# Moving one batch's query load, one transpose and two stores in the transfer order of a fused attention and MLP kernel

## Chip, core and metric

The kernel runs on one core of one Trainium2 chip. The metric is the device time of one launch in microseconds (us), taken several times; the median is the figure that is compared.

## What is computed

The reference is a linear attention without softmax, normalised per head, followed by a two-layer MLP with a sigmoid-approximated GELU:

```python
kv  = np.einsum('bhsd,bhse->bhde', k, v)          # b=8, h=8, s=576, d=64
out = np.einsum('bhsd,bhde->bhse', q, kv)
rms = np.sqrt(np.mean(out * out, axis=-1, keepdims=True) + 1e-06)
out = out / rms * g_norm
x = out.transpose(0, 2, 1, 3).reshape(4608, 512)
h = x @ w_in                                      # 512 x 2048
g = h * (1.0 / (1.0 + np.exp(-1.702 * h)))
return g @ w_out                                  # 2048 x 512, result float32
```

Inputs are float32 in HBM; the kernel computes in float16 with float32 sums.

## The kernel before

**Tiles and layers.** The 4,608 token rows are taken as nine tiles of 512 rows. Tiles 0 to 7 are the first 512 rows of batches 0 to 7; tile 8 gathers the remaining 64 rows of every batch. A loop over the tile number `t` (L982) writes one "layer" each time: both matrix products of the MLP for tile `t`, and, woven between their matmuls, the attention of batch `b = t + 1`, which yields the next layer's input `xT[b]`. The first product of a layer (L584 from layer 1 on) works through a list of steps; the second (L704) counts its 112 matmul positions `n` from 0 to 111. Layer 0 uses L473 and L819 with its own count. From layer 1 on both products use a seven-product scheme in place of eight block products.

**Order by hand.** The order is written out: `at1(i, f, ...)` hangs a call behind step `i` of the first product, `at2(n, f, ...)` behind position `n` of the second. Calls hung on one position run in the order in which they were hung. Each engine works through its own instructions in that order and waits where data is missing.

**Loads** are issued by GpSimd (POOL), which also casts float32 to float16 on the way; they use queue q0. `load_kv(b)` (L112) issues the 512 main rows of k and v into `kraw` and `vbuf`, then the 64 remaining rows of each. `load_q(b)` (L142) issues three transfers: the main rows of q, into `qbuf` for an odd batch and `qraw` for an even one, and two of 32 KB into `qrem[b % 2]`. There is one `kraw` and one `vbuf`, so k and v of the next batch can be loaded only when the products k-transposed times v (`kvp`, L247) of the batch before have read them.

**Turning.** SyncE (SP) issues DMA transposes, which go through queue q1 together with its stores. `transpose_q` (L288) turns q of batch b into `qTd`, of which there is one buffer; `transpose_rest` (L292) turns `qrem` into `qTr`. The products `outR` (L332, method `rows`) read `qTd`, the products `outT` of L306 read `qTr`. When the normalised result is in `x16`, `turn` (L359) multiplies it on VectorE and issues, after parts 1 and 3, a transpose into the next layer's `xT` (L368).

**Stores.** The result of tile `t` is collected in `osbs[t]`, with two buffers that alternate. Tiles 0 and 1 (`t < EARLY`) have another row order, so `store_early` (L838) issues eight transfers each of 64 to 192 KB, 1 MB in all, on SP; it is called at the end of `layers` (L797). Tiles 2 to 5 are stored in halves from within the second product (L692, L850), tiles 6 and 7 whole at the layer's end.

**Order around the change, before.**

| Where | What is hung there |
| --- | --- |
| layer 0, position 51 | clear the unused rows; `load_kv(2)`, second half of the heads and the remaining rows |
| end of layer 0 | `store_early(0)` on SP |
| layer 1, step 5 | `start(2)`, `transpose_q(2)`, `transpose_rest(2)` on SP |
| layer 1, step 22 | `load_kv(3)`, then `load_q(3)` |
| layer 1, positions 40, 50, 51, 52 | `turn` of batch 2, parts 0 to 3 |
| layer 1, positions 88 and 89 | k, v products of batch 3; `load_kv(4)`, `load_q(4)` |
| layer 1, position 100 | `transpose_q(3)`, `transpose_rest(3)` on SP |
| end of layer 1 | `store_early(1)` on SP |
| layer 2, position 15 | k, v products of batch 4, then `rows` of batch 3 |
| layer 2, positions 35, 38, 46, 48 | `turn` of batch 3 |
| layer 2, position 49 | `transpose_q(4)` on SP |
| layer 2, position 101 | v of batch 5 behind the end of batch 3's turning, q of batch 5 behind batch 4's `qTd` (POOL waits by a one-element copy, `mark`) |

Of the kernel before, what the change touches and what calls it, by code (L numbers as in the profile page):

```python
# [12 lines left out]
P = 128  # L13
# [3 lines left out]
def kernel(  # L17
# [10 lines left out]
    nc = tc.nc  # L28

    B, H, S, D = q.shape  # L30
# [7 lines left out]
    J = SM // P  # L38
    R = S - SM
    assert R == 64 and B * R == SM and KO == NPAIR and 2 * D == P  # L40
    NT = B + 1
    EARLY = 2
# [22 lines left out]
    qrem = [const.tile([P, 2, P], F16, name=f"qrem{i}") for i in range(2)]  # L65
# [71 lines left out]
    def q_rows(b):  # L137

        rows = qbuf if b % 2 else qraw.rearrange("p c x -> p (c x)")
        return rows[:, 0 : H * J * D]  # L140
# [14 lines left out]
    for n in "kqv":  # L155
# [11 lines left out]
        out=ident,  # L167
        in_=ident,
# [52 lines left out]
    class Attention:  # L221
# [63 lines left out]
                    r = slice(hl * D, (hl + 1) * D)  # L285
                    copy(self.engine, self.kb[to, c0:c1, half, 1 - hl], self.kvp[r, c0:c1, :])

        def transpose_q(self):  # L288
            self.qTd = attn.tile([P, H * J // 2, P], F16, name="qTd", tag="qTd", bufs=1)
            nc.sync.dma_start_transpose(out=self.qTd, in_=q_rows(self.b))  # L290

        def transpose_rest(self):  # L292
# [489 lines left out]
    def layers(t, units1, units2):  # L782
        hid = d0 if t == 0 else Hidden(t)
        seven = Seven(t, hid.gT) if t else None
        left = hid_seven(t, hid, seven, units1) if t else first_columns(hid, units1)
        osbs[t] = opool.tile([P, 4, DM], F32, name="osb", tag="osb")
        if t:
            todo = {n: [lambda x=x: seven.sums(*x) for x in xs] for n, xs in plan(t).later.items()}
            for n, us in units2.items():
                todo.setdefault(n, []).extend(us)  # L790
            for n, us in left.items():
                todo[n] = us + todo.get(n, [])
            seven.run(todo)
        else:
            project_all(hid.gT, units2)
        if t < EARLY:
            store_early(t)  # L797
        elif t < B and t not in HALVED:
            store(t, 0, J)

    def first_columns(hid, units):

        for i, fo in enumerate(COLS):
            if i >= GROUP:
                for ko in range(KO):
                    hid.mm(ko, fo)
                hid.gate(fo)
            for u in units.get(i, ()):
                u()
# [28 lines left out]
    def store_early(t):  # L838
        n = 0
        while n < SM:  # L840
            mo, j, p = n // P, n // PE_, n % PE_
            m = min((mo + 1) * P, (j + 1) * PE_) - n
            nc.sync.dma_start(
                out=out[t * S : (t + 1) * S, :][bass.DynSlice(NJ * p + j, m, step=NJ), :],
                in_=osbs[t][n % P : n % P + m, mo, :],
            )
            n += m

    def store(t, j0, j1):
        nc.sync.dma_start(  # L850
            out=out[t * S : t * S + SM, :].rearrange("(p j) m -> p j m", j=J)[:, j0:j1],
            in_=osbs[t][:, j0:j1],
        )
# [119 lines left out]
    def plan(t):  # L973
        return SECOND if t < EARLY else LATER if t < B - 1 else LAST_TWO

    HALVED = (2, 3, 4, 5)
# [5 lines left out]
    for t in range(NT):  # L982
        b = t + 1
        u1, u2 = {}, {}

        def at1(i, f, *args):
            u1.setdefault(i, []).append(lambda: f(*args))

        def at2(i, f, *args):
            u2.setdefault(i, []).append(lambda: f(*args))  # L990

        def of(b, name, *args):
            return lambda: getattr(live[b], name)(*args)

        if t == 0:
            for l in range(2):
                at1(6, nc.vector.memset, kvd[l], 0.0)
            at1(7, of(0, "out", NPAIR))
            at1(7, scale_w_in, 0, 4)
            at1(7, w_in_sums, 0, 2)  # L1000
            at1(8, start, 1)
            at1(12, scale_w_in, 4, 6)
            at1(12, w_in_sums, 2, 3)
            at1(13, load_q, 2)
            at2(4, setattr, a0, "ss_pool", Attention.ss_pool)
            at2(4, of(0, "ss", NPAIR, True))
            at2(4, of(0, "apply", NPAIR))
            at2(18, weight_sum, 0, 0, HF)
            at2(18, scale_w_in, 6, 8)
            at2(18, w_in_sums, 3, 4)  # L1010
            for c in range(NPAIR):
                at1(12, of(1, "pack_q", c))
                at2(9 + 3 * c, of(1, "q", c))
                at2((36, 36, 49, 49)[c], of(1, "kv", c))
                at2((41, 43, 54, 55)[c], of(1, "out", c))
                at2((45, 50, 58, 60)[c], of(1, "ss", c))
                at2((48, 52, 58, 62)[c], of(1, "apply", c))
            for n in range(1, 4):
                at2(19, weight_sum, n, 0, 4)
                at2(38, weight_sum, n, 4, 6)  # L1020
            at2(39, load_kv, 2, 0, H // 2, False)
            at2(51, clear_rest)
            at2(51, load_kv, 2, H // 2, H)

            def first_sum():
                made[1] = Sums(1, xT[1])
                made[1].form(0)

            at2(55, first_sum)
        elif b < B:  # L1030
            todo = plan(t)
            at = todo.attn
            if t == 1:
                at1(todo.steps.index("kv"), of(b, "kv_all", "D"))
                at1(5, start, b)
                at1(5, of(b, "transpose_q"))
                at1(5, of(b, "transpose_rest"))
                at1(4, nc.scalar.preload_act_table_set, "gelu_apprx_sigmoid_and_others")
                for n, i in ((1, 8), (2, 11), (3, 16)):
                    at1(i, weight_sum, n, 6, HF)  # L1040
                at1(22, load_kv, 3)
                at1(22, load_q, 3)
                at2(88, start, 3)
                at2(88, of(3, "kv_all", "A"))
                at2(89, load_kv, 4)
                at2(89, load_q, 4)
            elif t + 2 < B:
                at2(at["rows"][0], start, t + 2)
                at2(at["rows"][0], of(t + 2, "kv_products"))
                at2(52, of(t + 2, "kv_copies", "A"))  # L1050
                if t + 3 < B:
                    at2(at["rows"][0], load_kv, t + 3, 0, H, False, "k")
                    at2(101, after_turn, b)
                    at2(101, load_kv, t + 3, 0, H, True, "v")
                    at2(101, after_queries, t + 2)
                    at2(101, load_q, t + 3)
            if t + 2 < B:
                at2(49 if t > 1 else 100, of(t + 2, "transpose_q"))
                at2(100, of(t + 2, "transpose_rest"))
            at2(at["table"], nc.scalar.preload_act_table_set, "abs_reciprocal_sqrt_and_small")  # L1060
            for h in range(2):
                at2(at["roots"][h], of(b, "roots", h))
            for j in range(J):
                if j < J // 2:
                    at2(at["rows"][j], of(b, "rows", j))
                for name in ("add_up", "turn"):
                    at2(at[name][j], of(b, name, j))
            rest = (80, 90, 96, 97) if 1 < t < B - 2 else (46, 74, 80, 82)
            at2(rest[0], of(b, "out", NPAIR))
            at2(rest[1], of(b, "ss", NPAIR))  # L1070
            at2(rest[2], of(b, "apply", NPAIR))
            at2(rest[3], nc.scalar.preload_act_table_set, "gelu_apprx_sigmoid_and_others")
        elif t < B:
            for name in ("ss_pool", "rest_pool"):
                at2(16, setattr, live[1], name, (ps_a, "att"))
            at2(16, of(1, "out", NPAIR))
            at2(34, nc.scalar.preload_act_table_set, "abs_reciprocal_sqrt_and_small")
            at2(44, of(1, "ss", NPAIR))
            at2(50, of(1, "apply", NPAIR))
            at2(52, nc.scalar.preload_act_table_set, "gelu_apprx_sigmoid_and_others")  # L1080
        layers(t, u1, u2)


# [28 lines left out]
```

## Time and profile before

| What | Value |
| --- | --- |
| median of 3 runs | 259.14 us |
| lowest and highest | 258.35 and 259.88 us |
| the profiled execution's own time | 259.74 us |
| its span, first to last instruction | 258.0 us |
| mean granted TensorE clock | 0.993 of full speed |
| read from HBM, written | 36.70 MB, 9.44 MB |

The profile shows one execution. Its times are counted from the first instruction; 1.74 us of the profiled execution's time lie outside the span. Engines are PE (TensorE matmul), PEld (its weight loads), DVE (VectorE), ACT (ScalarE), POOL (GpSimd) and SP (SyncE). The layers stand in the chain of work as follows: layer 0 ends at 47.96 us, layer 1 at 75.30, layer 2 at 101.42, layer 3 at 127.54; later layers follow in steps of 26.1 to 24.5 us, and the last matmul ends at 254.30.

A row of a timeline gives start, duration, engine, line, operation and count. For a DMA this is the time its engine took to issue it, not that of the transfer. A row of DMA issues gives the size and, at its end, the time from issue to landing. A row of DMA queues gives packets, MB and the share of 16 engines' time in the stretch asked for; a share over 100% means that packets overlapped.

### The profile page before, as it was taken

How to read it: one execution, taken by the hardware profiler on the slowest of the kernel's cores; microseconds unless marked ns; L12 is line 12 of the kernel's file. 1: busy time of each engine (PE TensorE's matmuls, PEld its weight loads, DVE VectorE, ACT ScalarE, POOL GpSimd, SP SyncE). 2: the span in 40 equal slices, each digit the busy share in tenths (PEclk: the TensorE clock that was granted, in tenths of full speed). 3: DMA queues.
4: the chain of work that ended last, by engine and by line, in shares of the span. 5: the costliest groups of instructions: out<-in, count | busy, mean ns of one | idle time of the engine just before them, and what ended most of it. 6: DMA issues, size and time to landing. Idle time of an engine off the chain costs nothing.

```text
span 258.0 us, 6355 instructions
## 1 busy us (share of the span) xinstructions
PE 251.7 (98%) x2596; PEld 204.4 (79%) x2596; DVE 193.9 (75%) x344; ACT 177.1 (69%) x322; POOL 57.0 (22%) x92
## 2 busy tenths in 40 slices
PE   8899999999999999999999999999999999999994
PEld 2444454788888888888888888898888888888883
DVE  1546685899958986798679867987799787857872
ACT  3458743988758894899579957995799469536800
POOL 8773244208061013301150134000000000000013
PEclk9979999999999999999999999999999999999999
DMA  7999999999989979996999699909500430012005
GB/s 181 194 188 206 204 204 197 216 216 115 184 159 208 221 91 224 153 158 81 186 184 164 84 205 135 190 5 136 202 4 0 84 163 3 0 57 108 3 19 145
DMA packets 68687, 35.33 MB, mean 137 GB/s; under 512 B 37970, under 2 KB 66258, under 8 KB 68402
## 3 DMA queue, kind: packets, MB, share of 16 engines
q0 software_dynamic: 37632, 18.31, 55.3%
q1 hardware_dynamic: 30624, 16.29, 27.4%
q8 instruction: 20, 0.33, 0.5%
q10 hardware_dynamic: 402, 0.33, 0.5%
q14 instruction: 9, 0.07, 0.1%
HBM read 36.70 MB, written 9.44 MB: 179 GB/s over the span
## 4 chain that ended last, share of the span: by engine, by line
PE 93%; DMA 4%; issue 0%; POOL 0%; DVE 0%
PE o L704 38%; PE h L584 38%; PE hT L473 6%; PE o L819 5%; DMA vbuf<-in_v_dram 2%; DMA qraw<-in_q_dram 2%; PE kvp L247 2%; PE outR L332 1%; PE ss L379 1%; PE outT L302 1%; PE q L454 0%; PE kvp L259 0%; PE outT L306 0%; PE kv L259 0%; DVE osb L684 0%
## 5 line engine op out<-in xcount | busy, mean ns | idle before, releaser
L561 ACT ACTIVATE gT<-h 128x512 f16<-128x512 f32 x96 | 52.5, 601 | 5.6 <-PE h L584 5.6
L584 PEld LDWEIGHTS <-ws 128*128 128x128 f16 x512 | 50.1, 98 | 5.9
L704 PEld LDWEIGHTS <-gS 128*128 128x128 f16 x512 | 49.1, 98 | 6.1 <-DVE gS L636 0.3
L584 PE MATMUL h<-xS,ws 128*128 128x256 f16 x384 | 52.2, 273 | 0.0
L704 PE MATMUL o<-tw,gS 128*128 128x256 f16 x384 | 45.6, 273 | 0.0
L584 PEld LDWEIGHTS <-w_in_sb 128*128 128x128 f16 x384 | 37.4, 98 | 4.7
L704 PEld LDWEIGHTS <-gT 128*128 128x128 f16 x384 | 37.6, 98 | 4.3
L704 PE MATMUL o<-w_out_sb,gT 128*128 128x256 f16 x256 | 31.4, 273 | 0.0
L584 PE MATMUL h<-xT,w_in_sb 128*128 128x256 f16 x224 | 31.1, 272 | 0.0
L681 DVE TENSOR_TENSOR osb<-o,qf 128x512 f32<-128x512 f32 (+1 forms) x25 | 16.7, 669 | 11.7 <-PE o L704 11.7
L598 DVE TENSOR_TENSOR h<-h,s 128x512 f32<-128x512 f32 x32 | 22.2, 698 | 4.2 <-PE h L584 2.6
L600 DVE TENSOR_TENSOR s<-h,s 128x512 f32<-128x512 f32 x32 | 22.1, 691 | 4.1 <-PE h L584 3.3
L738 POOL DMA_DIRECT2D out_dram<-osb x6 | 3.2, 537 | 93.2 <-DVE osb L681 93.2
L636 DVE TENSOR_TENSOR gS<-gT 128x512 f16<-128x512 f16 (+2 forms) x32 | 21.3, 685 | 0.6 <-ACT gT L561 0.6
L561 ACT ACTIVATE gT<-s 128x512 f16<-128x512 f32 x32 | 19.8, 628 | 2.4 <-DVE s L600 2.3
L530 DVE COPY s<-h 128x512 f32<-128x512 f32 x19 | 13.0, 686 | 8.2 <-PE h L584 8.2
L584 PE MATMUL h<-xS,w_in_sb 128*128 128x256 f16 x128 | 18.9, 273 | 0.0
L115 POOL DMA_DIRECT2D kraw<-in_k_dram x7 | 6.0, 853 | 56.9 <-PE kvp L247 52.0
L348 DVE TENSOR_REDUCE sum<-sq 128x8 f32<-128x512 f16 x24 | 14.9, 678 | 4.7 <-ACT sq L342 4.7
L320 ACT ACTIVATE sq<-outT 128x512 f16<-128x512 f32 (+1 forms) x16 | 7.9, 495 | 15.1 <-PE outT L302 9.5
L990 ACT ACT_TABLE_LOAD x14 | 18.0, 1283 | 0.2
L381 ACT ACTIVATE rs<-ss,eps_t 128x512 f32<-128x512 f32 (+1 forms) x16 | 9.2, 582 | 12.4 <-PE ss L379 12.3
(104 smaller groups left out, 373.9 us busy)
## 6 DMA issues: line engine op xcount, KB each, us to landing
out_dram<-osb SPq DMA_DIRECT2D x8, 512.0 KB, 4.6
kraw<-in_k_dram POOLq DMA_DIRECT2D x5, 512.0 KB, 6.0
vbuf<-in_v_dram POOLq DMA_DIRECT2D x5, 512.0 KB, 10.4
out_dram<-osb SPq DMA_DIRECT2D x2, 1024.0 KB, 4.9
qraw<-in_q_dram POOLq DMA_DIRECT2D x3, 512.0 KB, 11.6
qbuf<-in_q_dram POOLq DMA_DIRECT2D x3, 512.0 KB, 10.4
out_dram<-osb SPq DMA_DIRECT2D x6, 192.0 KB, 5.9
w_in_sb<-in_moe_w_in_dram POOLq DMA_DIRECT2D x2, 512.0 KB, 10.1
```

The lines of the kernel that those rows point to most:

```text
L348: nc.vector.tensor_reduce(out=self.sum4[:, j, :], in_=self.o[j][1].rearrange("p (x d) -> p x d", d=D), op=ALU.add, axis=mybir.AxisListType.X,)
L473: nc.tensor.matmul(self.h[fo], w_in_sb[:, ko, fo * P : (fo + 1) * P], self.x[:, ko], start=(ko == 0), stop=(ko == KO - 1),)
L530: (nc.vector.tensor_copy if engine == "D" else nc.scalar.copy)(to, src)
L561: nc.scalar.activation(self.gT[:, to, n * TH : (n + 1) * TH], src, AFT.Gelu_apprx_sigmoid)
L584: nc.tensor.matmul(bank[name][:, a], w, x, start=(p in (1, 5) and a == 0 and k == 0), stop=(k == KH - 1), skip_group_check=True,)
L598: nc.vector.tensor_add(bank["z"], bank["x"], self.s5)
L600: nc.vector.tensor_add(self.s5, bank["x"], self.s5)
L636: op(s[:, n, lo], a, b)
L681: nc.vector.tensor_add(o, ps, self.kept[with_][:, m])
L704: nc.tensor.matmul(o, a, w, start=(p in (1, 2, 5) and i == 0 and (mo == 0 or split)), stop=(i == HF - 1), skip_group_check=True,)
L819: nc.tensor.matmul(os[mo], gT[:, fo, mo * P : (mo + 1) * P], w_out_sb[:, fo, :], start=(fo == 0), stop=(fo == FO - 1),)
L990: u2.setdefault(i, []).append(lambda: f(*args))
```

## The change

`load_q(3)` moves from layer 1, step 22, to layer 0, position 51, behind the last load of batch 2's k and v. `transpose_q(2)` gets a one-column copy on GpSimd ahead of it: it reads the last column of `qrem[1]`, which the last two transfers of `load_q(3)` fill, and writes into `qTd`, so the transpose, which overwrites `qTd`, comes behind it. `store_early(0)` moves from the end of layer 0 to layer 1, position 53, one behind the last part of batch 2's turning; `store_early(1)` moves from the end of layer 1 to layer 2, position 49, behind `transpose_q(4)`, which is hung on the same position earlier in the text. `at["turn"][J - 1] + 1` is 53 in layer 1 and 49 in layer 2.

```diff
-        def transpose_q(self):
+        def transpose_q(self, after=None):
             self.qTd = attn.tile([P, H * J // 2, P], F16, name="qTd", tag="qTd", bufs=1)
+            if after is not None:
+                nc.gpsimd.tensor_copy(out=self.qTd[0 : 2 * R, 0, 0:1], in_=after)
             nc.sync.dma_start_transpose(out=self.qTd, in_=q_rows(self.b))
...
-        if t < EARLY:
-            store_early(t)
-        elif t < B and t not in HALVED:
+        if EARLY <= t < B and t not in HALVED:
             store(t, 0, J)
...
             at2(51, load_kv, 2, H // 2, H)
+            at2(51, load_q, 3)
...
                 at1(5, start, b)
-                at1(5, of(b, "transpose_q"))
+                at1(5, of(b, "transpose_q", qrem[1][0 : 2 * R, 1, P - 1 : P]))
                 at1(5, of(b, "transpose_rest"))
...
                 at1(22, load_kv, 3)
-                at1(22, load_q, 3)
...
             at2(rest[3], nc.scalar.preload_act_table_set, "gelu_apprx_sigmoid_and_others")
+            if b - 2 < EARLY:
+                at2(at["turn"][J - 1] + 1, store_early, b - 2)
```

## The prediction

> **What bounds the kernel now.** I read the page first, then the sums by layer, the chain of waits, and last the timelines of the two engines that issue transfers.
>
> ```profile
> span 258.0 us, 6355 instructions
> PE 251.7 (98%) x2596; PEld 204.4 (79%) x2596; DVE 193.9 (75%) x344; ACT 177.1 (69%) x322; POOL 57.0 (22%) x92
> ```
>
> ```profile
> 47.96:75.30 27.34, 27.34 (x343) 23.67 (x342) 24.87 (x46) 21.93 (x41) 7.61 (x10) 1.00 1.25 182
> 75.30:101.42 26.12, 26.12 (x303) 23.27 (x302) 21.00 (x35) 20.59 (x39) 4.88 (x9) 1.00 1.13 173
> ```
>
> TensorE sets the time: in layers 1 and 2 its busy time (second number) equals the length of the stretch (first). No transfer ends a wait of TensorE there, so an earlier transfer buys nothing; a later one costs only if it passes its deadline. The deadlines are in the chain of waits:
>
> ```profile
> 63.33 0.57 PE outR L332 x32
> ...
> 67.12 0.12 PE outT L306 x4
> ...
> 71.93 0.75 PE kvp L247 x40
> ...
> 89.28 0.75 PE kvp L247 x40
> 90.03 0.57 PE outR L332 x32
> ...
> 115.41 0.75 PE kvp L247 x40
> ```
>
> These read `qTd` of batch 2 (63.33), `qTr` of batch 2 (67.12), k and v of batch 3 (71.93) and 4 (89.28), `qTd` of batch 3 (90.03), and k and v of batch 5 (115.41). Whatever comes after its time moves everything behind it, one for one, as TensorE has no idle time left to make it up.
>
> Next, SP's timeline and POOL's, with the landings of single transfers:
>
> ```profile
> 46.27 4.38 SPq L843 DMA_DIRECT2D out_dram<-osb  x8
> 51.40 4.26 SPq L290 DMA_TRANSPOSE qTd<-qraw  x1
> ...
> 68.74 3.26 SPq L368 DMA_TRANSPOSE xT<-x  x2
> 72.17 1.92 SPq L290 DMA_TRANSPOSE qTd<-qbuf  x1
> 74.27 1.73 SPq L294 DMA_TRANSPOSE qTr<-qrem  x1
> ...
> 98.19 2.10 SPq L290 DMA_TRANSPOSE qTd<-qraw  x1
> ```
>
> ```profile
> 46.35 0.69 POOL L120 DMA_DIRECT2D vbuf<-in_v_dram  x1 [0.41 <-DMA qrem<-in_q_dram]
> 58.20 0.88 POOL L115 DMA_DIRECT2D kraw<-in_k_dram  x1 [11.16 <-PE kvp L247]
> ...
> 60.76 0.69 POOL L120 DMA_DIRECT2D vbuf<-in_v_dram  x1
> 61.43 0.90 POOL L143 DMA_DIRECT2D qbuf<-in_q_dram  x1
> ...
> 72.95 0.90 POOL L115 DMA_DIRECT2D kraw<-in_k_dram  x1 [9.38 <-PE kvp L247]
> ...
> 75.38 0.72 POOL L120 DMA_DIRECT2D vbuf<-in_v_dram  x1
> ...
> 102.08 0.70 POOL L120 DMA_DIRECT2D vbuf<-in_v_dram  x1
> ```
>
> The remaining rows of v, the last of each batch's k and v, are the issues at 46.35 (batch 2), 60.76 (3), 75.38 (4) and 102.08 (5). How long they took to land stands at the end of the first four rows, in that order; then q of batch 3 (issued at 61.43), `qTd` of batch 2 (51.40) and `qTr` of batch 3 (74.27):
>
> ```profile
> vbuf<-in_v_dram POOLq DMA_DIRECT2D x1, 64.0 KB, 9.5
> ...
> vbuf<-in_v_dram POOLq DMA_DIRECT2D x1, 64.0 KB, 7.2
> ...
> vbuf<-in_v_dram POOLq DMA_DIRECT2D x1, 64.0 KB, 13.9
> ...
> vbuf<-in_v_dram POOLq DMA_DIRECT2D x1, 64.0 KB, 10.4
> ...
> qbuf<-in_q_dram POOLq DMA_DIRECT2D x1, 512.0 KB, 9.2
> ...
> qTd<-qraw SPq DMA_TRANSPOSE x1, 6.4
> ...
> qTr<-qrem SPq DMA_TRANSPOSE x1, 7.6
> ```
>
> The thing to see: batch 4 is complete at 75.38 + 13.9 = 89.28, the very time at which TensorE reaches it. Batch 3 has 71.93 - (60.76 + 7.2) = 4.0 us to spare, batch 5 115.41 - (102.08 + 10.4) = 2.9. So the place that can be hurt is the stretch from 72 to 89.
>
> Last, the queues: q0 carries the loads, q1 what SP issues. The stretches are 64 to 66 (loads alone), 72.5 to 76 (turnings alone), 79 to 81 (loads with a turning) and 82 to 86 (loads with a store):
>
> ```profile
> q0 software_dynamic: 758, 0.38, 142.3%
> ...
> q1 hardware_dynamic: 3260, 0.82, 115.1%
> ...
> q0 software_dynamic: 493, 0.25, 99.7%
> q1 hardware_dynamic: 268, 0.06, 30.4%
> ...
> q1 hardware_dynamic: 512, 0.84, 65.6%
> q0 software_dynamic: 601, 0.31, 55.6%
> ```
>
> From them come three prices. A store beside loads: in 4 us the loads moved 601 packets where alone they would move 2 x 758 = 1516; the 915 missing, at 2000/758 = 2.64 ns, are 2.4 us for 0.84 MB, so 3.0 us for the 1.05 MB of one tile. A turning alone: 3260 packets in 3.5 us, 1.1 ns each. A turning beside loads: 758 - 493 = 265 load packets lost, 0.70 us, for 268 packets, 2.6 ns each. One `qTd` with its `qTr` is 0.59 MB in packets of 0.25 KB (0.82 MB in 3260), some 2300: 2.5 us alone, 6.0 us beside loads.
>
> **The change, part by part.**
>
> **q of batch 3, loaded early.** Its three issues leave POOL's queue at 61.43 and follow the issue of 46.35, so the first goes out at 47.0; `qbuf` was last read by batch 1, whose products are over by then. Nothing on POOL stands behind them before 58.20, so the issue costs nothing. With the tile's store gone from this stretch, batch 2's last load lands up to 3.0 us before its 46.35 + 9.5 = 55.85; I take 52.85. Main q rows then add what they added behind batch 3's v, 61.43 + 9.2 - 67.96 = 2.7 us, and the 64 KB of `qrem` by bytes 0.3: landed at 55.85, or at 58.85 if the missing store gains nothing.
>
> **The wait ahead of batch 2's turning.** The trace has POOL copies of one element that serve the same end:
>
> ```profile
> 104.33 0.18 POOL L131 COPY mark<-qTd 1x1 f16<-1x1 f16 x1 [1.55 <-DMA qTd<-qraw]
> ```
>
> One column over 128 partitions I take at the same, 0.2; bounds 0 and 0.5, as no POOL copy here is larger. Behind it on POOL stands only the load of 58.20, which waits for `kvp` anyway; behind the transpose on SP stand the second transpose and then those of 68.74. The transpose goes out at 56.1 instead of 51.40. The earlier one, caught behind a store, needed 6.4 us to landing, so `qTd` is there at 62.5, 0.8 us ahead of 63.33. `qTr`, issued some 2.1 us later (98.19's row) with at most the 7.6 us of the row at 74.27, is there by 65.8, ahead of 67.12. Cost nothing; at the late bound of 58.85 `qTd` is 2.2 us late.
>
> **Batch 3's loads without q behind them** keep their 4.0 us of slack, less at most 0.7 for a `qTr` beside them (256 packets at 2.6 ns). The transposes of 68.74 get a free stretch. No gain: TensorE does not wait for either.
>
> **Tile 0's store, between batch 2's and batch 3's turning.** This is the costly part. Its eight issues take 4.38 us of SP and start when the second transpose of 68.74 is out, at 72.0. Batch 3's turning, queued behind them, goes out at 76.4 instead of 72.17.
>
> ```profile
> 58.00:60.00 2.00, 2.00 (x20) 1.79 (x19) 1.93 (x6) 1.76 (x4) 1.76 (x2) 1.00 0.09 13
> ```
>
> Before, it was over by 76: the row of 72.5 to 76 holds q1 alone, though k of batch 4 was issued at 72.95. Now it meets batch 4's loads. Batch 3's loads, alone, took 58.20 to 67.96, 9.8 us from first issue to last landing. So batch 4 alone would be in at 72.95 + 9.8 = 82.75. Before, 6.5 us came on top: the store 3.0, `qTr` 0.7, the held start 1.2 (no load packet before 76, 3.0 after the issue; batch 3's, issued at 58.20, began near 60, by the DMA share of 0.09 in the row below, so some 1.8 after), and 1.6 that I can't place. After: the store 2.2 (it starts about 1 us ahead of the loads and so has 0.3 of itself done), `qTd` and `qTr` 6.0: 90.95, which is 1.7 us after 89.28. The bounds of this: a turning at its alone price, 2.5, gives 87.5, no cost; the store at its full 3.0 and the 1.6 again give 93.35, a cost of 4.1. I take 1.7, since loads and turning side by side are what the row of 79 to 81 shows. `qTd` itself, 2048 packets at 268 per 2 us, would take 15.3: 76.4 + 15.3 = 91.7, also 1.7 after its 90.03, so the two delays are one. Behind it on SP is only `qTr`, due at layer 2's end.
>
> The Trainium skill, DMA: Bandwidth & Descriptors, section on queues, rings and completion order, says that each engine takes turns between the queues that have work, packet by packet. The rows of 79 to 81 and 82 to 86 look like it; that of 72.5 to 76, with no load packet in it, does not. By that rule the 1.7 stands; by the other row alone it would be nothing.
>
> **Tile 1's store, behind batch 4's turning.** It leaves the start of layer 2, where the first 3.0 of the sum above stood for it, and goes out from 98.19 + 2.10 = 100.3. It is then in front of tile 2's first half and batch 4's `qTr`, which is due only at layer 3's end, and beside v of batch 5. That batch's last load is late by 3.0 at most: 112.48 + 3.0 = 115.48, 0.1 after 115.41. Bounds 0 and 1.7 (the unplaced 1.6 again). I take 0.1. The result buffers are no bound: tile 0's is next written in layer 2,
>
> ```profile
> 97.12 1.38 DVE L681 TENSOR_TENSOR osb<-o,qf 128x512 f32<-128x512 f32 x2
> ```
>
> some 18 us after its store, and tile 1's a layer later still.
>
> **Sum.** 1.7 + 0.1 = 1.8 us. The profiled execution took 259.74 (258.0 of span, 1.74 around it), so 261.54; it lay 0.6 above the median of 259.14, so on the median 260.9.
>
> **The rivals.**
>
> *The queues take turns in long stretches* (the not-slower side). If a busy q1 keeps q0 from starting, as from 72.95 to 76, tile 0's store and batch 3's turning run through first and the loads follow undisturbed: 72.95 + 9.8 + 2.2 + 2.5 = 87.45, even with the 1.6 at 89.05, before 89.28. It decides where the loads' first packets come after 79. For it speaks that row; against it, that SP needs 4.38 us to issue 1.05 MB, so q1 has gaps. Price 0.1 from layer 3: 259.2.
>
> *Batch 2's `qTd` late in layer 1.* If q of batch 3 lands at 57.5 rather than 55.85, the 0.8 us of slack is gone and 0.8 is lost; at 58.85, 2.2. The row of 46.35 speaks for the store having been the cause of the lateness, so I think it unlikely. With layer 2 in time: 260.4.
>
> *The unplaced 1.6 us returns.* If it belongs to every start of loads under a busy q1, layer 2 loses 1.7 + 1.6 and layer 3 its 0.1: 3.4, so 262.5. For it speaks that the old stretch had it; against it, that its store and `qTr` came one after the other there, so part of it may be theirs.
>
> *A gain.* Layer 1 is 27.34 long, layer 2 26.12; 0.75 of the difference is its second `kvp` group. The remaining 0.47 is all that earlier transfers could win: 258.7. TensorE shows no wait that it would be won from.
>
> **How the numbers follow.** Forecast 0.50, turns in stretches 0.25, layer 1 late 0.09, the unplaced time 0.10, gain 0.06. Within 0.5%, 1.3 us, which is about what a measurement of this kernel can tell from no change, fall nearly all of the second, half of the last, and a fifth of the forecast where its 1.7 shrinks toward 1.0; slower are four fifths of the forecast, the third at two thirds and the fourth: 0.40 + 0.06 + 0.10 = 0.56, some more for causes unnamed, 0.60. Faster 0.05, same 0.35. The range goes from 258.7, the gain's time, to 263.2, the upper bound of 4.1 in layer 2; the forecast's own is 260.2 (the store half done before the loads begin, which leaves 1.0) to 263.2.
>
> **What would show it.** Right: in the profile after, a gap in TensorE of 1 to 3 us ahead of the first `kvp` of layer 2, released by a load of batch 4, with q0 and q1 sharing the stretch from 78 to 88; the turning of batch 3 issued near 76; no gap at `outR` in layer 1; under 0.5 us ahead of `kvp` in layer 3. Wrong: batch 4's last load landing by 89 with turnings alone on the queues before 80, or a gap at 63 in layer 1, or layers 1 to 3 of unchanged length.

## The result and the profile after

The changed kernel took 261.33 us in the median of 21 runs (260.06 to 265.03), the kernel before, on the same chips, 259.52 (258.33 to 260.54). The ratio is 1.0078, 95% interval 1.0062 to 1.0094: 2.0 us slower. Two single executions, 265.03 us here and 266.20 us in e3 below, lie more than 1.5% above the fastest of their kernel and are not in the ratios. The profiled execution of the changed kernel took 261.27 us, close to the median, and has a span of 259.5. Most line numbers from L290 on are two higher in it (L332 is L334 there); those of the stores are as before.

First the busy times by layer. The columns are the stretch, its length, then busy time and count of PE, PEld, DVE, ACT and POOL, granted clock, DMA share and GB/s:

```profile
47.56:74.90 27.34, 27.34 (x343) 23.65 (x342) 24.91 (x46) 21.93 (x41) 7.67 (x11) 1.00 1.16 141
74.90:102.96 28.06, 26.38 (x303) 23.37 (x302) 21.05 (x36) 20.60 (x39) 4.98 (x9) 1.00 1.20 165
102.96:129.09 26.13, 26.13 (x304) 23.27 (x302) 20.45 (x34) 20.60 (x39) 4.47 (x7) 1.00 1.13 182
```

Layer 1 is as long as before (27.34), layer 3 too (26.13); layer 2 has grown from 26.12 to 28.06. All of the loss in this execution, 1.94 us, is there, and TensorE's busy time shows that it waited. (It began layer 1 at 47.56 instead of 47.96, which hides 0.4 of the loss in the span. In e4 and e5 below layer 1 begins at 46.5 and 46.6; why this start varies was not looked into.) TensorE's timeline says for what:

```profile
88.81 0.32 PE L247 MATMUL kvp<-vbuf,kraw 128*64 128x64 f16 x8
89.52 0.69 PE L247 MATMUL kvp<-vbuf,kraw 128*64 128x64 f16 x32 [0.39 <-DMA vbuf<-in_v_dram]
91.51 0.64 PE L334 MATMUL outR<-kvd,qTd 64*128 64x64 f16 x32 [1.29 <-DMA qTd<-qbuf]
```

The batch 4 products pause 0.39 for the remaining rows of v; then `outR` of batch 3 waits 1.29 for its turned q. The larger wait is the second one, and it ends last. SP's timeline shows why that is late:

```profile
56.57 1.78 SPq L292 DMA_TRANSPOSE qTd<-qraw  x1
58.45 1.82 SPq L296 DMA_TRANSPOSE qTr<-qrem  x1
68.34 3.55 SPq L370 DMA_TRANSPOSE xT<-x  x2
71.93 5.64 SPq L843 DMA_DIRECT2D out_dram<-osb  x8
77.68 7.08 SPq L292 DMA_TRANSPOSE qTd<-qbuf  x1
84.93 1.31 SPq L296 DMA_TRANSPOSE qTr<-qrem  x1
```

The eight transfers of tile 0's store hold SP from 71.93 to 77.57, and batch 3's turning goes out at 77.68 where it went out at 72.17 before. Issuing it then takes 7.08 us instead of 1.92. POOL's timeline has the other side:

```profile
56.35 0.19 POOL L291 COPY qTd<-qrem 128x1 f16<-128x1 f16 x1 [6.81 <-DMA qrem<-in_q_dram]
...
72.55 0.89 POOL L115 DMA_DIRECT2D kraw<-in_k_dram  x1 [10.72 <-PE kvp L247]
...
74.98 0.71 POOL L120 DMA_DIRECT2D vbuf<-in_v_dram  x1
...
103.53 0.70 POOL L120 DMA_DIRECT2D vbuf<-in_v_dram  x1
```

Batch 4's loads start at 72.55, 5 us ahead of the turning. The landings, of the last loads of batches 4 (74.98) and 5 (103.53), and of batch 2's `qTd` and `qTr`:

```profile
vbuf<-in_v_dram POOLq DMA_DIRECT2D x1, 64.0 KB, 14.5
...
vbuf<-in_v_dram POOLq DMA_DIRECT2D x1, 64.0 KB, 12.2
...
qTd<-qraw SPq DMA_TRANSPOSE x1, 5.4
...
qTr<-qrem SPq DMA_TRANSPOSE x1, 6.8
```

Batch 4 was in at 89.5, 0.2 later than before, though TensorE was 0.4 earlier. Lastly the queues in the stretch from 85 to 91:

```profile
q0 software_dynamic: 1898, 0.56, 84.9%
q1 hardware_dynamic: 1893, 0.48, 61.0%
```

Over these 6 us both queues moved nearly the same number of packets, 1898 and 1893. The counts fit the turn-taking, packet by packet, that the Trainium skill describes (DMA: Bandwidth & Descriptors, queues, rings and completion order). The start of a turning, in e7 below, looks different.

### The profile page after: what moved, and what is told of

Read it like the earlier page. It is cut to its first block, busy times and chain, and to the rows that moved or that the text cites. A ratio compares the mean times of both kernels' runs of the same rounds, so it can differ in the third digit from the quotient of the medians.

```text
span 259.5 us, 6356 instructions
## 1 busy us (share of the span) xinstructions
PE 250.5 (97%) x2596; PEld 203.8 (79%) x2596; DVE 194.3 (75%) x344; ACT 177.1 (68%) x322; POOL 57.5 (22%) x93
## 3 DMA queue, kind: packets, MB, share of 16 engines
q1 hardware_dynamic: 30624, 16.29, 28.9%
## 4 chain that ended last, share of the span: by engine, by line
PE 78%; DMA 15%; POOL 4%; issue 1%; DVE 0%; POOLq 0%
PE o L706 37%; PE h L586 34%; DMA vbuf<-in_v_dram 6%; DMA qTd<-qbuf 5%; DMA w_in_sb<-in_moe_w_in_dram 3%; PE o L819 2%; PE kvp L247 1%; POOL w_in_sb L180 1%; PE outR L334 1%; POOL qraw L91 1%; POOL kraw L91 1%; POOL vbuf L91 1%; PE ss L381 1%; PE kvp L259 0%; PE outT L304 0%
## 5 line engine op out<-in xcount | busy, mean ns | idle before, releaser
L350 DVE TENSOR_REDUCE sum<-sq 128x8 f32<-128x512 f16 x24 | 14.9, 679 | 6.6 <-ACT sq L344 6.6
L383 ACT ACTIVATE rs<-ss,eps_t 128x512 f32<-128x512 f32 (+1 forms) x16 | 9.2, 582 | 11.4 <-PE ss L381 11.4
```

The costliest lines, as they stand in the source:

```text
L350: nc.vector.tensor_reduce(out=self.sum4[:, j, :], in_=self.o[j][1].rearrange("p (x d) -> p x d", d=D), op=ALU.add, axis=mybir.AxisListType.X,)
L383: nc.scalar.activation(rs[:, 0:n], t[:, 0:n], AFT.Abs_reciprocal_sqrt, bias=eps_t, scale=1.0 / D)
```

## The experiments

Two theories stood at the start. **Order**: batch 3's turning, issued behind the store, falls among batch 4's loads. **Volume**: tile 0's megabyte in the stretch from 72 to 89 is too much, wherever it stands there. The first four kernels take the change apart.

### e1: tile 0's store behind the turning

```diff
-                at2(at["turn"][J - 1] + 1, store_early, b - 2)
+                at2(101 if t == 1 else at["turn"][J - 1] + 1, store_early, b - 2)
```

> The changed kernel, with tile 0's store hung behind batch 3's turning (position 101 of layer 1) instead of ahead of it; all else of the change stays. Order theory (batch 3's turning, issued behind the store, falls among batch 4's loads): the turning goes out near 72 and is over by 77, layer 2 is 26.1 to 26.3 long, the median is that of before, ratio 0.998 to 1.001. Volume theory (the store of tile 0 in the stretch from 72 to 89 is itself too much, wherever it stands): layer 2 stays 27.5 to 28.1 long, ratio 1.005 to 1.008.

Measured: 259.48 us against 259.13, ratio 1.0016 (0.9998 to 1.0034). The profile by layer, batch 3's turning on SP, and one row of TensorE's timeline:

```profile
47.00:75.55 28.55, 27.35 (x344) 23.70 (x342) 24.86 (x46) 21.93 (x41) 7.68 (x11) 1.00 1.19 143
75.55:101.67 26.12, 26.12 (x303) 23.27 (x302) 21.06 (x36) 20.58 (x39) 4.94 (x9) 1.00 1.16 175
```

```profile
72.70 2.03 SPq L292 DMA_TRANSPOSE qTd<-qbuf  x1
```

```profile
63.57 0.64 PE L334 MATMUL outR<-kvd,qTd 64*128 64x64 f16 x32 [1.20 <-DMA qTd<-qraw]
```

The turning goes out 2.85 us ahead of layer 2's start again, and layer 2 is back at 26.12 with the same bytes in the stretch, so volume is out. A second thing shows that the changed kernel's own profile did not: layer 1 lost 1.2 us, waiting for batch 2's `qTd`. Here it took 7.0 us from issue to landing, where the changed kernel's took 5.4.

### e2 and e6: tile 0's store alone

The kernel before, with `store_early(0)` hung at position 53 of layer 1 and nothing else moved:

```diff
-        if t < EARLY:
+        if t == 1:
             store_early(t)
...
+            if t == 1:
+                at2(at["turn"][J - 1] + 1, store_early, 0)
```

> The kernel before, with only tile 0's store moved to position 53 of layer 1; q of batch 3, its turning and tile 1's store as before. Order theory: this part alone gives the loss, layer 2 27.8 to 28.6 long, ratio 1.006 to 1.010; tile 1's store then comes behind batch 3's turning, after 86, and harms batch 4's loads by 0.5 at most. Rival (the loss needs the early q of batch 3 or tile 1's late store): layer 2 under 26.5 long.

Measured: 259.96 against 259.13, ratio 1.0032 (1.0019 to 1.0046), half of what was expected. In the profile layer 2 was 27.74 long, but the profiled execution, 261.68 us, was the slowest of the eleven. TensorE waited there twice:

```profile
90.64 0.69 PE L247 MATMUL kvp<-vbuf,kraw 128*64 128x64 f16 x32 [0.78 <-DMA vbuf<-in_v_dram]
91.92 0.64 PE L332 MATMUL outR<-kvd,qTd 64*128 64x64 f16 x32 [0.59 <-DMA qTd<-qbuf]
```

The same kernel was then measured again, beside the changed one:

> e2 once more (only tile 0's store moved), with more rounds, on the same chip as the changed kernel. If tile 0's store were the whole of the loss: ratio within 0.0015 of the changed kernel's. If the early q of batch 3 with its wait adds a part of its own in layer 1: ratio 1.002 to 1.005, some 0.8 to 1.3 us below the changed kernel.

Measured: 260.16 against 259.23, ratio 1.0044 (1.0019 to 1.0068), and in its profile:

```profile
74.39:101.57 27.18, 26.38 (x304) 23.37 (x302) 20.58 (x34) 20.59 (x39) 4.05 (x8) 1.00 1.34 197
```

```profile
90.12 0.64 PE L332 MATMUL outR<-kvd,qTd 64*128 64x64 f16 x32 [0.76 <-DMA qTd<-qbuf]
```

The store alone makes the same use late: in both profiles `outR` starts when the turned q arrives. In e2's profile batch 4's loads were late too, and held TensorE 0.78 before that; so the loads' deadline, on which the prediction laid the weight, can be missed as well. The store alone costs about 1 us (0.8 and 0.9 by the medians, 1.06 by this profile): about half of the loss. The ratio lies where the second case of the expectation has it, but the changed kernel's profiles, here and in e5, show no loss in layer 1 that would make up the rest.

### e3: the early q with its wait, alone

Both stores as before; `load_q(3)` early and the copy ahead of `transpose_q(2)` as in the change.

> The kernel before, with only q of batch 3 loaded early and batch 2's turning waiting for it; both stores as before. Step of the prediction: with the store in the way q of batch 3 lands at 58 to 59 and qTd of batch 2 at 64 to 66, so layer 1 is 1 to 3 us longer, ratio 1.004 to 1.011. Rival (the wait has slack): layer 1 27.3 to 27.6, ratio under 1.002. Layer 2 in both 26.1 to 26.3.

Measured: 262.14 in the median of three runs (261.09 to 262.98) against 259.13, ratio 1.0112 (1.0079 to 1.0145). POOL's copy that waits for q of batch 3, and TensorE's timeline:

```profile
59.51 0.19 POOL L291 COPY qTd<-qrem 128x1 f16<-128x1 f16 x1 [9.76 <-DMA qrem<-in_q_dram]
```


```profile
64.31 0.64 PE L334 MATMUL outR<-kvd,qTd 64*128 64x64 f16 x32 [1.17 <-DMA qTd<-qraw]
...
69.37 0.28 PE L308 MATMUL outT<-qTr,kvd 128*128 128x64 f16 x4 [1.29 <-DMA qTr<-qrem]
```

Beside tile 0's store q of batch 3 arrives 3.2 us later than in the changed kernel (59.51 against 56.35). Both turned parts of batch 2's q then come late, and TensorE waits 2.5 us for them together. With tile 0's store still in its old place the wait for q of batch 3 is the dearest part of the three.

### e4 and e9: tile 1's store alone

The kernel before, with only `store_early(1)` hung at position 49 of layer 2.

> The kernel before, with only tile 1's store moved behind batch 4's turning in layer 2. Step of the prediction: batch 4's last load lands some 3 us sooner, at 86, which gains nothing; batch 5's lands up to 3 us later, 1 us ahead of or at its product; layers 2 and 3 both 26.1 to 26.3, ratio 0.998 to 1.001. Rival (the late store costs layer 3 its slack): layer 3 26.6 to 27.8.

Measured: 259.00 against 259.13, ratio 0.9983 (0.9957 to 1.0009). Layers 1 to 3 were 27.34, 26.12 and 26.13 long. The last load of batch 4, POOL's timeline and landing:

```profile
73.94 0.71 POOL L120 DMA_DIRECT2D vbuf<-in_v_dram  x1
```

```profile
vbuf<-in_v_dram POOLq DMA_DIRECT2D x1, 64.0 KB, 9.5
```

83.4, against a use that this execution reaches at 87.84: 4.4 us of slack where there had been none. Whether that is worth something was asked again:

> e4 once more (only tile 1's store moved), with more rounds. If batch 4's loads were late in some executions of the kernel before, where they land at the very time of their use, their 4 us of slack shows: ratio 0.996 to 0.999, and this is the version that beats both. If not: 0.999 to 1.001.

Measured: 258.80 against 259.00, ratio 0.9995 (0.9979 to 1.0012). The interval reaches 1, so no gain is shown. Its profile shows what the slack in layer 2 is paid with:

```profile
114.58 0.69 PE L247 MATMUL kvp<-vbuf,kraw 128*64 128x64 f16 x32 [0.42 <-DMA vbuf<-in_v_dram]
```

With tile 1's store beside batch 5's loads, layer 3 can now lose a few tenths, as it did here; in e4's profile it lost nothing.

### e5: the changed kernel again

> The changed kernel itself, beside the others of this set on one chip. Both theories: ratio 1.006 to 1.010; layer 2 27.5 to 28.2 long in its profile. What its profile decides: if batch 2's qTd is late by up to 1.2 us in some executions, as it was in e1, layer 1 is longer than 27.34 here too; if not, the loss is in layer 2 alone.

Measured: 261.18 against 259.23, ratio 1.0088 (1.0055 to 1.0121). TensorE's timeline in its profile:

```profile
88.35 0.69 PE L247 MATMUL kvp<-vbuf,kraw 128*64 128x64 f16 x32 [0.17 <-DMA vbuf<-in_v_dram]
90.41 0.64 PE L334 MATMUL outR<-kvd,qTd 64*128 64x64 f16 x32 [1.37 <-DMA qTd<-qbuf]
```

Layer 1 was 27.34, layer 2 27.91 long. The same two waits as in the first profile, none in layer 1. This execution, 260.16 us, was the fastest of the seven, 1.0 below their median; so it does not rule out that layer 1 is late in slower ones.

### e7: a late turning with no store near it

e4, with batch 3's turning taken from position 100 of layer 1 to step 2 of layer 2, gated by a small copy on VectorE:

```diff
+            if gate:
+                nc.vector.tensor_copy(out=self.qTd[:, 0, 0:1], in_=ident[:, 0:1])
...
+            if t == 2:
+                at1(2, of(3, "transpose_q", True))
+                at1(2, of(3, "transpose_rest"))
```

> e4 (only tile 1's store moved) with batch 3's turning held to step 2 of layer 2, near 77, by a one-column copy on VectorE; no store lies in the stretch from 72 to 98. It prices the turning among loads by itself. If it costs 2.6 ns a packet (6.0 us of the loads' time), batch 4's last load lands 15.5 to 16.5 us after the first issue, against 11.9 in e4, and qTd between 86 and 89: both just in time, layer 2 26.1 to 26.6, ratio 0.998 to 1.003. If the turning alone were the whole of the loss, layer 2 is 27.5 or more. If it runs as one block at 1.1 ns, batch 4 lands at 13 to 14.5.

Measured: 259.83 against 259.23, ratio 1.0023 (0.9995 to 1.0052). SP's timeline, the loads' queue from 76.3 to 80.3 (no row of q1 stands beside it), layer 2, and TensorE's timeline:

```profile
76.24 5.49 SPq L292 DMA_TRANSPOSE qTd<-qbuf  x1
```

```profile
q0 software_dynamic: 1503, 0.70, 138.2%
```

```profile
74.49:102.07 27.58, 26.13 (x303) 23.24 (x301) 20.99 (x36) 20.60 (x39) 4.89 (x9) 1.00 1.16 137
```

```profile
90.68 0.64 PE L334 MATMUL outR<-kvd,qTd 64*128 64x64 f16 x32 [1.45 <-DMA qTd<-qbuf]
```

This is the run that told most. For four microseconds after its issue the turning moved not one packet, while q0 moved batch 4's loads. Then both shared: from 82 to 83 each moved 202 packets. In the changed kernel batch 2's turning, issued at 56.57 with no loads about, had moved its first 106 packets by 58.0. A busy q0 alone does not explain the long start: the transposes into `xT` of this same execution, issued from 67.93 on while batch 3's loads ran out, were under way 2 us later with q0 at work beside them,

```profile
q1 hardware_dynamic: 441, 0.11, 137.4%
q0 software_dynamic: 481, 0.07, 96.4%
```

as this row of 69 to 70 shows. Whether the late turning had packets waiting behind the loads for those 4 us, or SP (which took 5.49 us to issue it) had not yet given it any, the trace does not tell.

From issue to use the turning took 14.4 us, as long as with the store ahead, and `outR` waited 1.45 in this execution. Batch 4's last load, issued at 74.58, landed 11.4 later at 86.0, 13.8 after the first issue, well ahead of its use. So two of the expected numbers fell: the loads lose less to the turning than 6.0 us (13.8 is 4.0 above the 9.8 that batch 3's loads took), and the turning loses more. That a late turning costs time without a store near it is shown by this profile alone: layer 2 was 27.58 long, but the execution, 261.33 us, was the second slowest of ten. It also lost 0.68 in layer 3, waiting for batch 5's v beside tile 1's store. The median shows a smaller loss, and its interval reaches to nothing.

### e8: no wait ahead of batch 2's turning

e1 without the copy:

```diff
-                at1(5, of(b, "transpose_q", qrem[1][0 : 2 * R, 1, P - 1 : P]))
+                at1(5, of(b, "transpose_q"))
```

> e1 without the copy, so batch 2's turning does not wait for q of batch 3. If the wait is what made qTd of batch 2 late in e1: the turning is issued near 46.5, lands at 56 to 61, no wait at outR in layer 1, batch 2's last load at 55 to 56.5 against 57.2 needed, ratio 0.997 to 1.000. If the wait protects batch 2's loads: TensorE waits 0.5 to 2 us ahead of batch 2's kvp, ratio 1.002 to 1.008.

Measured: 259.41 against 259.23, ratio 1.0001 (0.9972 to 1.0031). No wait at `outR` in layer 1 now, but one ahead of it:

```profile
56.77 0.69 PE L247 MATMUL kvp<-vbuf,kraw 128*64 128x64 f16 x32 [0.34 <-DMA vbuf<-in_v_dram]
```

The turning, issued at 45.96, runs beside batch 2's loads, and these come 0.3 late. Both halves of the expectation are partly true. In these two profiles the wait costs 1.20 (e1) and its absence 0.34 (e8), but the medians of e1 and e8 can't be told apart.

### e10: half of the store ahead

Four of the eight transfers at position 53, four at 101:

```diff
-                at2(at["turn"][J - 1] + 1, store_early, b - 2)
+                half = SM // 2 if t == 1 else SM
+                at2(at["turn"][J - 1] + 1, store_early, b - 2, 0, half)
+                at2(101, store_early, b - 2, half)
```

> The changed kernel with four of the eight transfers of tile 0's store ahead of batch 3's turning and four behind it. In the five profiles where the turning went out among batch 4's loads it landed 13.6 to 14.4 us after its issue, store or no store ahead, and outR needs it 14.7 us after the start of layer 2. The turning here is issued 2.6 us sooner, near the start of layer 2. Issue-time theory: it lands 13.3 to 14.2 after that start, layer 2 is 26.1 to 26.3 long, ratio 1.000 to 1.003 (as e1). Theory of the store's bytes in the stretch (1 MB there as before): layer 2 stays 27 or longer, ratio 1.004 to 1.008.

Measured: 259.86 against 259.00, ratio 1.0034 (1.0010 to 1.0057). SP's timeline, the turning's landing, layer 2, and TensorE in layer 1:

```profile
74.96 7.28 SPq L292 DMA_TRANSPOSE qTd<-qbuf  x1
```

```profile
qTd<-qbuf SPq DMA_TRANSPOSE x1, 14.9
```

```profile
75.33:101.64 26.31, 26.31 (x304) 23.37 (x302) 21.00 (x35) 20.60 (x39) 4.99 (x9) 1.00 1.29 176
```

```profile
63.36 0.64 PE L334 MATMUL outR<-kvd,qTd 64*128 64x64 f16 x32 [0.78 <-DMA qTd<-qraw]
```

Layer 2 is at 26.31, just above what the issue-time theory has, and not at 27. The turning landed at 89.86, in time; the 0.2 too much lies in the `kvp` group of batch 4, whose last load landed only at 75.41 + 14.1 = 89.5. Layer 1 has lost 0.78, where e1 lost 1.20, which is most of what the median shows. The ratio is a little above the range given for it.

### The seven profiles in one table

Times in us. Lead is the issue of batch 3's turning less the start of layer 2; outR is the start of batch 3's `outR` less the start of layer 2, which is 14.73 where nothing is late.

| Kernel | Lead | Issue to outR | outR | Late |
| --- | --- | --- | --- | --- |
| before | 72.17 - 75.30 = -3.1 | turned by 76 | 14.73 | 0 |
| e10 | 74.96 - 75.33 = -0.4 | 14.9 to landing | 14.93 | 0.2, by batch 4's loads |
| e7 | 76.24 - 74.49 = 1.75 | 14.4 | 16.19 | 1.5 |
| e6 | 76.42 - 74.39 = 2.03 | 13.7 | 15.73 | 1.0 |
| e2 | 77.88 - 75.63 = 2.25 | 14.0 | 16.29 | 1.6 |
| after | 77.68 - 74.90 = 2.78 | 13.8 | 16.61 | 1.9 |
| e5 (after) | 76.74 - 73.95 = 2.79 | 13.7 | 16.46 | 1.7 |

Once batch 4's loads are running, the turning needs 13.7 to 14.9 us, whatever went ahead of it on SP: the whole store, half of it or nothing. In all five profiles in which `outR` was late by 1 us or more it started on the arrival of the turned q, so there the moment of issue decides the loss. With 13.7 to 14.9 us of way, the last moment that would do lies between 0.2 before and 1.0 after the start of layer 2.

None of the kernels tried beats the kernel before by more than its interval; the nearest, e4 and its repetition e9, are at 0.9983 and 0.9995, and both intervals hold 1.

## Why the prediction was right

The forecast was 1.8 us more than before; measured are 1.8 by the medians and 2.0 by the ratio. The mechanism was the one named, tile 0's store pushing batch 3's turning in among batch 4's loads; of the two waits that follow from it, the prediction had the larger one at the wrong use.

**What bounds, and the deadlines.** Right. In no profile did an earlier transfer shorten layers 1 to 3, and the waits of TensorE that make the losses stand at the uses named, except e8's, at `kvp` of batch 2.

**q of batch 3.** Predicted to land at 55.85 without the store in the way, measured 56.2 (the copy that waits for it starts at 56.35). The late bound, 58.85, is e3's case (59.51 there).

**The wait ahead of batch 2's turning.** Predicted issue 56.1, `qTd` 62.5, `qTr` 65.8; measured 56.57, 62.0 and 65.2, both in time in the two profiles of the changed kernel. The slack of 0.8 was rightly called thin: e1 and e10 show it used up, by 1.20 and 0.78. This is the rival given a chance of 0.09. It shows in two kernels that share this part with the changed one, and in neither profile of the changed kernel itself.

**Tile 0's store ahead of batch 3's turning.** Predicted 1.7 us in layer 2, measured 1.94 and 1.8 in two profiles. The 1.7 of the sum was worked out from the loads, and that term was mis-sized: the store and the turning were to add 2.2 + 6.0 = 8.2 us to the 9.8 that the loads take alone, and batch 4's last load was to land at 90.95. From its first issue at 72.55 to its landing at 89.5 it took 16.9, so 7.1 were added, and it kept TensorE only 0.39. In e7, without the store, the turning added 4.0 where the prediction has 6.0.

The turning itself is the later of the two. The prediction set its landing beside the first sum, at 91.7, and called the two delays one; `outR` began at 91.51. That this second estimate fits is in part luck, since two errors cancel: the turning went out at 77.68 and not at 76.4, as the store held SP for 5.64 and not 4.38, and it then took 13.8 and not 15.3. Nor did it go at the even pace assumed, 268 packets in 2 us: in e7 it moved none for 4 us, and from 85 to 91 in the changed kernel q1 moved 1893 packets in 6 us.

So of the signs named for being right, the main one did not come: the gap ahead of layer 2's first `kvp`, put at 1 to 3 us, was 0.39 and 0.17, and the larger one stood at `outR`. The others came: the turning issued near 76 (77.68 and 76.74), both queues at work from 78 to 88, no gap at `outR` in layer 1, none ahead of `kvp` in layer 3.

**The rival of queues in long stretches** was half right as a description. In e7 one queue did run alone for 4 us, but it was that of the loads, and the turning came after: the side that makes the loss and not the one that avoids it.

**Tile 1's store.** Predicted 0.1 in layer 3; 0 in the changed kernel, whose batch 5 landed at 103.53 + 12.2 = 115.7 ahead of 116.95, as layer 2's loss had moved the deadline; 0.42 in e9, 0.68 in e7.

**Two figures that do not follow.** 3.0 us less three tenths of it is 2.1, not the 2.2 of the sum. The 260.4 of a late layer 1 is worked out nowhere; its own 0.8 to 2.2 on 259.14 give 259.9 to 261.3. Neither changes the forecast.

**What is left open.** Tile 0's store alone costs about 1 us, the whole change 2.0. In the profiles the turning goes out 0.5 to 0.75 later in the changed kernel than in e2 and e6, and layer 1 can add up to 1.2 in some executions. Together these could be of the right size, but how often layer 1 is late in the changed kernel was not measured; its two profiles, of an execution near the median and of the fastest of seven, show none. Why a turning issued among the loads needs 13.7 us and more stays open as well; the runs show only that it does.

## What to carry to other kernels

When TensorE has no idle time, look for the transfers that land at the very time of their use, and ask of a moved store not how many bytes it moves but what stands behind it on the issuing queue. Here a DMA transpose that went out at 72.17, just ahead of a batch of loads, was over by 76; the same one issued among them took 13.7 us and more, so it is the store that should wait, not the transpose. Read the loss by layer in the profile: e2 and e10 have nearly the same ratio (1.0032 and 1.0034), one from layer 2 and the other mostly from layer 1.

## What the runs showed of the hardware that was not expected

Around some DMA transposes the queues come nearly to a halt for 1 us or more. In the changed kernel, by half microseconds (the last column is GB/s):

```profile
70.00:70.50 0.50, 0.50 (x8) 0.44 (x6) 0.50 (x2) 0.46 (x1) 0.00 (x0) 1.00 5.34 106
70.50:71.00 0.50, 0.50 (x7) 0.42 (x5) 0.50 (x2) 0.48 (x2) 0.00 (x0) 1.00 0.00 0
71.00:71.50 0.50, 0.50 (x7) 0.27 (x7) 0.50 (x2) 0.50 (x1) 0.00 (x0) 1.00 0.04 4
71.50:72.00 0.50, 0.50 (x35) 0.50 (x36) 0.18 (x1) 0.31 (x1) 0.00 (x0) 1.00 0.08 9
72.00:72.50 0.50, 0.50 (x21) 0.44 (x16) 0.00 (x0) 0.17 (x1) 0.00 (x0) 1.00 1.01 224
```

The transposes into `xT`, issued at 68.34 and 69.62, moved next to nothing for 1.5 us. Loads are not needed for it: q0 moved no packet from 69 to 74 here. Nor is it a part of the change: the kernel before has 11 and 9 GB/s in the two half microseconds from 71 to 72. In e7 it shows among loads, with both queues slow: 33 and 12 GB/s in the two half microseconds from 84.5 to 85.5. The packets that started just before have long durations (a DMA share of 5.34). No run here tells its cause, and it was not tried to avoid it.
